# The last output store of a GELU MLP kernel, issued by two engines in two halves of its rows

## The chip, the core and the metric

The kernel runs on one core of a Trainium2 chip. The metric is the device time of one execution in microseconds (us); where several runs are given, their median counts. A core has engines that run side by side and synchronise by semaphores: TensorE (PE, matrix multiplies), VectorE (DVE), ScalarE (ACT), GpSimd (POOL) and SyncE (SP). SP, ScalarE and GpSimd can issue DMAs. An issue occupies the issuing engine's queue for a moment, and the data then moves on DMA engines, 16 for this core, which in this kernel raise a semaphore by 16 for each finished transfer.

## What is computed

The reference is a two-layer perceptron on 2048 tokens with 448 features and 1792 hidden units, in bfloat16:

```python
B, S, D, F = 1, 2048, 448, 1792
h = jnp.einsum("bsd,df->bsf", x, w1) + b1
h = _gelu(h)                       # tanh approximation
return jnp.einsum("bsf,fd->bsd", h, w2) + b2
```

## The kernel before

**Tiles and stages.** Tokens are cut into 4 chunks of 512 and the hidden units into 14 tiles of 128. The first layer (`l1`, matmuls at L260) computes for each pair of chunk and hidden tile a PSUM bank of 128 x 512 sums. ScalarE applies bias and GELU to each of the 56 banks (L360) and writes `g_sb`. The second layer (`l2`, matmuls at L334) takes 16 token tiles of 128 rows in order; for each it adds up 14 matmuls into one PSUM bank of 128 x 448. VectorE adds the bias `b2` to each finished bank (L382) and writes `out_sb`, raising the semaphore `sem_osb` by one.

**The list of outputs.** `outs` holds one entry for each token tile, except that the last tile is cut in two by columns: 0 to 320 and 320 to 448. There are therefore 17 entries. Each is one group of 14 matmuls, one VectorE add and one store. The last entry has 128 columns of 128 rows, in bfloat16 32 KB.

**Loads.** SP issues most of the loads at the start (L204, L205, L178, L183 to L187, L197, L191, L213); ScalarE issues `b1` (L349) and one piece of `w1` (L178), and GpSimd a small filler (L227). All of them are issued before the second layer begins.

**The order of the stores.** The helper `store` (L164 to L167) issues the DMA of one entry from `out_sb` to the output and has it raise `sem_od` by 16. `sync_work` (L203 to L217) has SP wait for each add in turn and issue the first 16 stores:

```python
for n in range(len(outs) - 1):
    sp.wait_ge(sem_osb, n + 1)
    store(sp, n)
sp.wait_ge(sem_od, 16 * len(outs))
```

The last line (L217) is the kernel's final wait: SP waits until all 17 stores have landed, 17 times 16 = 272. The seventeenth store is at the end of `scalar_work`, behind ScalarE's last activation (L364, L365):

```python
act.wait_ge(sem_osb, len(outs))
store(act, len(outs) - 1)
```

So every engine's order is fixed by its program text, and across engines only the semaphores order the work.

Of the kernel before, what the change touches and what calls it, by code (L numbers as in the profile page):

```python
# [11 lines left out]
def bass_standalone__dense_activation_gelu__prompt_kernel(  # L12
# [10 lines left out]
    P = 128  # L23
    HALF = P // 2
# [89 lines left out]
    outs = [(j, 0, D) for j in range(NST - 1)] + [(NST - 1, 0, OCUT), (NST - 1, OCUT, D)]  # L114
# [6 lines left out]
    with ExitStack() as es:  # L121
# [12 lines left out]
        out_sb = sb("out_sb", [P, NST, D], BF16)  # L134
# [22 lines left out]
        sem_osb = S_("sem_osb")  # L157
        sem_od = S_("sem_od")
# [2 lines left out]
        x0_view = x2[0:SC, :].rearrange("(p t) d -> p t d", t=STC)  # L161
        out0_view = out2[0:SC, :].rearrange("(p t) d -> p t d", t=STC)

        def store(eng, n):  # L164
            j, c0, c1 = outs[n]
            to = out0_view[:, j, c0:c1] if j < STC else out2[j * P:(j + 1) * P, c0:c1]
            eng.dma_start(to, out_sb[:, j, c0:c1]).then_inc(sem_od, 16)  # L167

        def x_part(n, parts):
            h, k = parts[0]  # L170
            to = xT_sb[:, k:k + len(parts), 2 * h * P:2 * (h + 1) * P]
            src = ps[XBANK[n]][:, 0:2 * P * len(parts)]
            return to, src.rearrange("p (k t) -> p k t", k=len(parts))

        def load_w10(eng, i):
            a, b = W0_PIECES[i]
            with nc.allow_non_contiguous_dma(reason="w1 column pieces"):
                eng.dma_start(w1_sb[:, 0, a * P:b * P], w1[0:P, a * P:b * P]).then_inc(sem_w10[i], 16)  # L178

        def load_w1(eng):  # L180
            with nc.allow_non_contiguous_dma(reason="w1 column pieces"):
                for k, r in list(enumerate(KROW))[1:]:
                    eng.dma_start(w1_sb[:, k, 0:WCUT], w1[r:r + P, 0:WCUT]).then_inc(sem_w1[k], 16)  # L183
                eng.dma_start(
                    w1_sb[:, 0:3, WCUT:F], w1[0:3 * P, WCUT:F].rearrange("(k p) f -> p k f", p=P)
                ).then_inc(sem_w1r, 16)
                eng.dma_start(w1_sb[:, 3, WCUT:F], w1[KROW[3]:D, WCUT:F]).then_inc(sem_w1r, 16)  # L187

        def load_w2(eng, i):
            a, b = W2_PIECES[i]  # L190
            eng.dma_start(  # L191
                w2_sb[:, a:b, :], w2[a * P:b * P, :].rearrange("(ft p) d -> p ft d", p=P)
            ).then_inc(sem_w2[i], 16)

        def load_xT(eng, c):
            for k, d0 in enumerate(KROW):
                eng.dma_start(  # L197
                    xT_sb[:, k, c * SC:(c + 1) * SC],
                    x2[c * SC:(c + 1) * SC, d0:d0 + P],
                    transpose=True,  # L200
                ).then_inc(sem_x[c], 16)

        def sync_work(sp):  # L203
            sp.dma_start(xn_sb[:, 0:2, :], x0_view[:, 0:2, :]).then_inc(sem_xn[0], 16)  # L204
            sp.dma_start(xn_sb[:, 2:4, :], x0_view[:, 2:4, :]).then_inc(sem_xn[1], 16)  # L205
            load_w10(sp, 1)
            load_w1(sp)
            load_xT(sp, 1)
            for c in range(2, NSC):
                load_xT(sp, c)  # L210
            for i in range(len(W2_PIECES)):
                load_w2(sp, i)
            sp.dma_start(b2_bc[:, :], b2.partition_broadcast(P)).then_inc(sem_b2, 16)  # L213
            for n in range(len(outs) - 1):
                sp.wait_ge(sem_osb, n + 1)
                store(sp, n)
            sp.wait_ge(sem_od, 16 * len(outs))  # L217

        def gpsimd_work(pool):
            pool.memset(ident[:, :], 0.0).then_inc(sem_id, 1)  # L220
# [127 lines left out]
        def scalar_work(act):  # L348
            act.dma_start(b1n_sb[0:NFT, :], b1.rearrange("(c p) -> c p", p=P)).then_inc(sem_b1n, 16)  # L349
            load_w10(act, 0)  # L350
            zero = nc.const_aps.tensor(0.0, [P, 8], FP32)
            act.activation(act_junk[:, :], zero, ACT.Gelu_apprx_tanh)  # L352
            for n, (e, parts) in enumerate(XPARTS):
                if e == "a":
                    act.wait_ge(sem_xtp, n + 1)
                    act.copy(*x_part(n, parts)).then_inc(sem_xTa, 1)  # L356
            act.wait_ge(sem_b1, 1)
            for i, (c, ft) in enumerate(order):
                act.wait_ge(sem_l1, i + 1)
                act.activation(  # L360
                    g_sb[:, ft, c * SC:(c + 1) * SC], bank("g", i)[:, :], ACT.Gelu_apprx_tanh,
                    bias=b1_f[:, ft:ft + 1], scale=1.0,
                ).then_inc(sem_g, 1)
            act.wait_ge(sem_osb, len(outs))  # L364
            store(act, len(outs) - 1)  # L365

        def vector_work(dve):
            for n, (e, parts) in enumerate(XPARTS):
# [17 lines left out]


        sync_work(nc.sync)
        gpsimd_work(nc.gpsimd)
        tensor_work(nc.tensor)  # L390
        scalar_work(nc.scalar)
        vector_work(nc.vector)

# [27 lines left out]
```

## Time and profile before

| what | value |
|---|---|
| median of 3 runs | 94.05 us |
| the runs | 93.27, 94.05, 94.05 us |
| the profiled execution, its own time | 94.23 us |
| its span, first to last instruction | 92.9 us |
| granted TensorE clock | 1.000 |
| second layer's matmuls, L334 | 238, 42.6 us busy, mean 341 ns |
| VectorE's adds, L382 | 17, 10.2 us busy, mean 597 ns |
| store issues on SP, L167 | 16, from 52.0 to 90.8 us, median 332 ns |
| store issue on ScalarE, L167 | 1, at 91.4 us, 358 ns |
| SP's final wait for the landings, L217 | 1.7 us |

How to read it: the span is a part of the execution's own time; 94.23 - 92.9 = 1.33 us lie around it. A row of the timeline begins with the start in us from the span's start and the length in us, then the engine (SPq and ACTq are the DMA issues of SP and ScalarE), the line of the kernel, the operation, and output <- input. A row of the DMA issues ends with how many there were, the KB of each, and the median us from the start of the issue to the landing. In the windows a row begins with the stretch and its length; then come the busy times of PE, PE's weight loads, DVE, ACT and POOL, the granted clock, the busy share of the 16 DMA engines, and the GB/s that they moved. A DMA queue's row has its packets, MB and share of the 16 engines' time: q1 is the queue of SP's DMAs, q10 that of ScalarE's.

### The profile page before, as it was taken

The page shows a single profiled execution, that of the slowest core. Times are in us where ns is not written, and L with a number is a line of the kernel's source. Part 1 is how long each engine was busy: PE and PEld are TensorE (multiplying, and loading weights), DVE is VectorE, ACT ScalarE, POOL GpSimd, SP SyncE. Part 2 cuts the span into 40 slices and gives each one's busy share as a digit, 9 for nine tenths or more (in the row PEclk, how much of TensorE's full clock was granted, in tenths as well). Part 3 has the DMA queues.
Part 4 walks back from the last instruction along what each step waited for, and adds up shares of the span by engine and source line. Part 5 has one row for each costly group of instructions (what it writes and reads, how often), then busy time and mean ns, then how long its engine had stood idle before and what let it go on. Part 6 is the DMA issues. An engine that isn't in the chain of part 4 may idle for free.

```text
span 92.9 us, 1487 instructions
## 1 busy us (share of the span) xinstructions
PE 89.3 (96%) x650; PEld 47.5 (51%) x650; DVE 12.2 (13%) x25; ACT 36.7 (40%) x61; POOL 1.4 (1%) x7
## 2 busy tenths in 40 slices
PE   6968999999999999999999999999999999999991
PEld 4743445555555555555545555555555555555571
DVE  0260000000000000000000222222122222221132
ACT  2640599879777887779776000000000000000000
POOL 5000000000000000000000000000000000000000
DMA  1989965655991000000000110111111101111111
GB/s 34 326 296 347 188 132 96 75 108 91 308 375 46 0 0 4 7 0 0 0 0 0 49 46 10 49 49 49 49 49 49 42 9 55 49 49 49 49 49 49
DMA packets 12562, 7.52 MB, mean 81 GB/s; under 512 B 7171, under 2 KB 12172, under 8 KB 12556
## 3 DMA queue, kind: packets, MB, share of 16 engines
q1 hardware_dynamic: 12208, 7.26, 29.6%
q10 hardware_dynamic: 316, 0.17, 0.6%
q8 instruction: 5, 0.08, 0.3%
q0 software_dynamic: 32, 0.00, 0.0%
q14 instruction: 1, 0.01, 0.0%
HBM read 4.02 MB, written 1.84 MB: 63 GB/s over the span
## 4 chain that ended last, share of the span: by engine, by line
PE 90%; DMA 5%; SPq 1%; DVE 0%; issue 0%
PE ps L334 46%; PE ps L260 44%; DMA wi_sb<-in_w_dram 5%; SPq L178 0%; SPq L205 0%; SPq L204 0%; DVE out_sb L382 0%
## 5 line engine op out<-in xcount | busy, mean ns | idle before, releaser
L260 PE MATMUL ps<-xT_sb,wi_sb 64*128 64x512 bf16 (+2 forms) x384 | 43.0, 374 | 1.0 <-DMA wi_sb<-in_w_dram 1.0
L334 PE MATMUL ps<-wo_sb,g_sb 128*128 128x448 bf16 (+2 forms) x238 | 42.6, 341 | 0.0
L360 ACT ACTIVATE g_sb<-ps,bi_f 128x512 bf16<-128x512 f32 x56 | 33.7, 695 | 10.7 <-PE ps L260 10.7
L334 PEld LDWEIGHTS ps<-wo_sb,g_sb 128*128 128x128 bf16 x238 | 22.7, 98 | 20.1 <-issue 0.4
L260 PEld LDWEIGHTS ps<-xT_sb,wi_sb 64*128 64x128 bf16 (+1 forms) x384 | 21.8, 94 | 21.5 <-DMA wi_sb<-in_w_dram 1.5
L382 DVE TENSOR_TENSOR out_sb<-ps,bo_bc 128x448 bf16<-128x448 f32 (+2 forms) x17 | 10.2, 597 | 74.9 <-PE ps L334 74.9
L233 PE MATMUL ps<-const-bfloat16-1.0 128*128 128x256 bf16 x12 | 2.7, 417 | 0.8 <-PEq L406 0.8
L233 PEld LDWEIGHTS ps<-const-bfloat16-1.0 128*128 128x128 bf16 x12 | 1.7, 144 | 1.4 <-issue 0.8
L352 ACT ACT_TABLE_LOAD x1 | 1.3, 1283 | 1.8 <-issue 1.8
L356 ACT CAST xT_sb<-ps 128x512 bf16<-128x512 f32 (+1 forms) x3 | 1.5, 515 | 1.1 <-PE ps L243 1.1
L371 DVE CAST xT_sb<-ps 128x256 bf16<-128x256 f32 x3 | 1.2, 420 | 4.1 <-PE ps L243 4.1
L243 PE MATMUL ps<-ident,xn_sb 128*128 128x128 bf16 x16 | 1.6, 257 | 0.0
L243 PEld LDWEIGHTS ps<-ident,xn_sb 128*128 128x128 bf16 x16 | 1.3, 117 | 0.4 <-issue 0.4
L376 DVE STREAM_TRANSPOSE bit_sb<-bin_sb 32x32 bf16<-32x32 bf16 x4 | 0.8, 200 | 0.1
L227 POOL DMA_DIRECT2D bin_sb<-in_w_dram x1 | 0.7, 657 | 0.2 <-issue 0.2
L222 POOL TENSOR_SCALAR_AFFINE_SELECT ident<-ident 128x128 bf16<-128x128 bf16 x1 | 0.3, 288 | 0.2 <-POOL ident L220 0.2
L352 ACT ACTIVATE act_junk<-const-float32-0.0 128x8 bf16<-128x8 f32 x1 | 0.2, 209 | 0.0
L220 POOL MEMSET ident<- 128x128 bf16 x1 | 0.2, 204 | 0.3 <-POOLq L406 0.3
L378 DVE CAST bi_f<-bit_sb 128x14 f32<-128x14 bf16 x1 | 0.2, 175 | 0.0
L406 POOL MEMSET const-bfloat16-1.0<- 128x1 bf16 x1 | 0.1, 102 | 0.0
L406 POOL MEMSET const-uint8-127<- 128x1 uint8 x1 | 0.1, 102 | 0.0
L406 POOL MEMSET const-float32-0.0<- 128x1 f32 x1 | 0.1, 98 | 0.2 <-issue 0.2
(1 smaller groups left out, 0.1 us busy)
## 6 DMA issues: line engine op xcount, KB each, us to landing
out_dram<-out_sb SPq DMA_DIRECT2D x15, 112.0 KB, 1.7
wo_sb<-in_w_dram SPq DMA_DIRECT2D x2, 784.0 KB, 5.8
wi_sb<-in_w_dram SPq DMA_DIRECT2D x3, 256.0 KB, 5.2
wi_sb<-in_w_dram SPq DMA_DIRECT2D x1, 576.0 KB, 6.4
xn_sb<-in_x_dram SPq DMA_DIRECT2D x2, 224.0 KB, 2.7
wi_sb<-in_w_dram SPq DMA_DIRECT2D x1, 192.0 KB, 6.5
xT_sb<-in_x_dram SPq DMA_TRANSPOSE x12, 4.2
wi_sb<-in_w_dram ACTq DMA_DIRECT2D x1, 128.0 KB, 3.0
```

Source lines behind the costliest of these rows:

```text
L227: pool.dma_start(b1n_sb[NFT:SQ, :], w1[0:SQ - NFT, 0:P]).then_inc(sem_b1x, 16)
L233: pe.matmul(ps[0][:, 0:WN], lhsT=ones_w, rhs=ones_x, start=True, stop=True)
L243: mm = pe.matmul(ps[XBANK[n]][:, col:col + P], lhsT=xn_sb[:, 2 * h + t, KROW[k]:KROW[k] + P], rhs=ident[:, :], start=True, stop=True,)
L260: return pe.matmul(bank("g", i)[:, t0:t1], lhsT=w1_sb[lo:hi, k, ft * P:(ft + 1) * P], rhs=xT_sb[lo:hi, k, c * SC + t0:c * SC + t1], start= ...
L334: mm = pe.matmul(bank("o", n)[:, 0:c1 - c0], lhsT=g_sb[:, ft, j * P:(j + 1) * P], rhs=w2_sb[:, ft, c0:c1], start=(ft == 0), stop=(ft == NF ...
L352: act.activation(act_junk[:, :], zero, ACT.Gelu_apprx_tanh)
L356: act.copy(*x_part(n, parts)).then_inc(sem_xTa, 1)
L360: act.activation(g_sb[:, ft, c * SC:(c + 1) * SC], bank("g", i)[:, :], ACT.Gelu_apprx_tanh, bias=b1_f[:, ft:ft + 1], scale=1.0,).then_inc( ...
L371: dve.tensor_copy(*x_part(n, parts)).then_inc(sem_xTd, 1)
L376: dve.transpose(b1t_sb[to, :], b1n_sb[:, to]).then_inc(sem_b1T, 1)
L382: dve.tensor_tensor(out=out_sb[:, j, c0:c1], in0=bank("o", n)[:, 0:c1 - c0], in1=b2_bc[:, c0:c1], op=ALU.add,).then_inc(sem_osb, 1)
L406: nc = _bacc.Bacc("TRN2", target_bir_lowering=False, num_devices=1)
```

## The change

The helper `store` takes a range of rows, with all 128 as the default. The first 16 stores are issued as before. Of the seventeenth, SP issues rows 0 to 63 and ScalarE rows 64 to 127; both wait for the same add, the seventeenth rise of `sem_osb`. There are now 18 stores in all, and SP's final wait counts to 18 times 16 = 288.

```diff
-        def store(eng, n):
+        def store(eng, n, p0=0, p1=P):
             j, c0, c1 = outs[n]
             to = out0_view[:, j, c0:c1] if j < STC else out2[j * P:(j + 1) * P, c0:c1]
-            eng.dma_start(to, out_sb[:, j, c0:c1]).then_inc(sem_od, 16)
+            eng.dma_start(to[p0:p1], out_sb[p0:p1, j, c0:c1]).then_inc(sem_od, 16)
...
                 sp.wait_ge(sem_osb, n + 1)
                 store(sp, n)
-            sp.wait_ge(sem_od, 16 * len(outs))
+
+            sp.wait_ge(sem_osb, len(outs))
+            store(sp, len(outs) - 1, 0, HALF)
+            sp.wait_ge(sem_od, 16 * (len(outs) + 1))
...
             act.wait_ge(sem_osb, len(outs))
-            store(act, len(outs) - 1)
+            store(act, len(outs) - 1, HALF, P)
```

## The prediction, made before the changed kernel was run

> **What bounds the kernel now.** I read four views in this order: the page's head and chain of waits, the timeline of the last three microseconds, the windows over the stores' packets, and the timeline of the first two microseconds, where SP and ScalarE already issue DMAs side by side.
>
> The page's head and the chain come first, because they say what a microsecond in any place is worth.
>
> ```profile
> span 92.9 us, 1487 instructions
> PE 89.3 (96%) x650; PEld 47.5 (51%) x650; DVE 12.2 (13%) x25; ACT 36.7 (40%) x61; POOL 1.4 (1%) x7
> ```
>
> ```profile
> 7.20 41.33 PE ps L260 x374
> 48.53 42.53 PE ps L334 x238
> 91.06 0.02 issue
> 91.08 0.29 DVE out_sb L382
> ```
>
> TensorE is the chain from 7.20 to 91.06 us without a break. After it stand one VectorE add of 0.29 us and then the flight of the last store, which the chain does not print but the span contains: the add ends at 91.08 + 0.29 = 91.37 and the span at 92.9. The edit touches nothing before 91.37 us. So the whole stake is the last 1.53 us, 1.6% of 94.05.
>
> The timeline of the tail, and the rows of the DMA issues (KB each, us to landing), show who issues what there.
>
> ```profile
> 90.30 0.49 DVE L382 TENSOR_TENSOR out_sb<-ps,bo_bc 128x320 bf16<-128x320 f32 x1 [1.28 <-PE ps L334]
> 90.82 0.33 SPq L167 DMA_DIRECT2D out_dram<-out_sb  x1
> 91.08 0.29 DVE L382 TENSOR_TENSOR out_sb<-ps,bo_bc 128x128 bf16<-128x128 f32 x1 [0.29 <-PE ps L334]
> 91.40 0.36 ACTq L167 DMA_DIRECT2D out_dram<-out_sb  x1
> ```
>
> ```profile
> out_dram<-out_sb SPq DMA_DIRECT2D x15, 112.0 KB, 1.7
> out_dram<-out_sb SPq DMA_DIRECT2D x1, 80.0 KB, 1.6
> out_dram<-out_sb ACTq DMA_DIRECT2D x1, 32.0 KB, 1.5
> ```
>
> Both stores are issued 0.03 us after their add (90.79 to 90.82 on SP, 91.37 to 91.40 on ScalarE), so neither queue has a backlog. SP's issue ends at 90.82 + 0.33 = 91.15, and from there SP does nothing but wait for the landings; its waits give 1.7 us for that (91.15 to about 92.9). ScalarE's store lands 1.5 us after its issue begins: 91.40 + 1.5 = 92.9, the end of the span.
>
> The windows of 0.1 us split that 1.5 us (last columns: clock, DMA share, GB/s).
>
> ```profile
> 92.00:92.10 0.10, 0.00 (x0) 0.00 (x0) 0.00 (x0) 0.00 (x0) 0.00 (x0) 1.00 0.03 6
> 92.10:92.20 0.10, 0.00 (x0) 0.00 (x0) 0.00 (x0) 0.00 (x0) 0.00 (x0) 1.00 0.00 0
> 92.20:92.30 0.10, 0.00 (x0) 0.00 (x0) 0.00 (x0) 0.00 (x0) 0.00 (x0) 1.00 0.14 36
> 92.30:92.40 0.10, 0.00 (x0) 0.00 (x0) 0.00 (x0) 0.00 (x0) 0.00 (x0) 1.00 0.87 192
> 92.40:92.50 0.10, 0.00 (x0) 0.00 (x0) 0.00 (x0) 0.00 (x0) 0.00 (x0) 1.00 0.47 98
> ```
>
> The last store's packets move from about 92.2 to 92.5. Before them lie 0.8 us from the start of the issue to the first packet, and behind them 0.4 us until the landing is seen. Only about 0.3 of the 1.5 us is data; 1.2 us is a fixed part that any store pays. The 80 KB store's packets are over by 92.1, so SP's queue is empty before the last rows move.
>
> **The change part by part.**
>
> *Removed:* rows 0 to 63 (16 KB) from ScalarE's store. The fixed 1.2 us stays on both halves, since each is a store of its own. What fewer bytes save I take from the three sizes: (1.7 - 1.5) us over (112 - 32) KB is 0.0025 us a KB, so 16 KB less is worth -0.04 us. The best end: if the time of the packets went with the rows of each queue alone, half of 0.3 us would go, -0.15 us; and if the issue of 0.36 us also went with the rows, another -0.18. The rows speak against the second: an issue of 448 columns and one of 320 both take 0.33 us, and ScalarE's 1 KB-wide load took 0.365 against 0.358 for its store. No row here has 64 partitions, so the end of the range stays at -0.33 us. I take -0.04, because the same 32 KB cross the same engines, which are 87% busy at their peak.
>
> On this point the Trainium skill, page "DMA: Bandwidth & Descriptors", section "Rules for kernel authors", advises against two transfers of disjoint partition halves, since both are spread over the same 16 DMA engines and so serialize. The trace's 87% share in the peak window fits it; by the rule the -0.04 us would be nothing, and the sum would be 0.04 us higher.
>
> *Added on SP, wait and issue:* SP gets a wait for the seventeenth add and one DMA issue. SP is free from 91.15, the add is ready at 91.37, so the new wait replaces 0.25 us of the wait for landings. The issue of 0.33 us (the row of the 80 KB store) then stands at 91.40 to 91.73 beside ScalarE's at 91.40 to 91.76 and is not added to it: SP's cover is its final wait until 92.9, behind which nothing is queued. Were that cover gone, SP's own issue would be 0.33 us on the path. SP's half by itself would land at 91.40 + 1.5 - 0.04 = 92.86, with ScalarE's.
>
> *Added, two issues at the same instant:* both engines are released by the same add, which before happened at no store. The nearest rows are at the start.
>
> ```profile
> 0.75 0.66 ACTq L349 DMA_DIRECT2D bin_sb<-in_b_dram  x1
> 1.44 0.36 ACTq L178 DMA_DIRECT2D wi_sb<-in_w_dram  x1
> ...
> 0.75 0.39 SPq L204 DMA_DIRECT2D xn_sb<-in_x_dram  x1
> 1.20 0.41 SPq L205 DMA_DIRECT2D xn_sb<-in_x_dram  x1
> 1.66 0.42 SPq L178 DMA_DIRECT2D wi_sb<-in_w_dram  x1
> ```
>
> They disagree. ScalarE's issue at 1.44 overlaps two of SP's (1.20 to 1.61, 1.66 to 2.08) and took 0.365 us, 0.007 more than the lone one at the end: about +0.01 us. The issues at 0.75 start together, and ScalarE's took 0.66 us, 0.30 more. But that one is also the first DMA of its queue and has 14 rows, so its length has three possible causes; the row at 1.44 has the tile shape of 128 rows and a warm queue. I take +0.01 and keep +0.30 as the upper end; full exclusion would be +0.36, ScalarE's whole issue.
>
> *Added, one more completion:* a store of 128 rows left 144 packets, the 16 above its rows being, I read, what raises the semaphore by 16. So the tail has 16 packets more, one on each of 16 engines. In the window from 90.5 to 93.5 us this queue's row is
>
> ```profile
> q10 hardware_dynamic: 144, 0.03, 5.0%
> ```
>
> and 5.0% of 16 engines' 3.0 us, over 144 packets, is 0.017 us each: +0.02 us. The lower end is nothing.
>
> *Moved:* the final wait counts to 288 and not 272, in the same place; it frees no buffer. No instruction of PE, VectorE or the activations is added or moved, and no load is.
>
> *Sum:* -0.04 + 0.01 + 0.02 = -0.01 us. The profiled execution took 94.23 us, of which 92.9 is the span and 1.33 lies around it; its sum is 94.22. It stands 0.18 us above the median of the runs shown, 94.05, so on that median the sum is 94.04, which I give as 94.0.
>
> **The rivals.**
>
> *The issues exclude each other.* Place: 91.40 us, where one add releases two issues. Price: +0.30 us (0.66 - 0.36) instead of +0.01, so 94.04 + 0.29 = 94.33, say 94.3; it decides if the second issue is held until the first is nearly through. For it speaks the pair at 0.75; against it the overlap at 1.44 at no cost. It would be slower, but by 0.3%.
>
> The Trainium skill, page "Perfetto Trace Analysis", section "DMA Instruction — HWDGE (DVE, Sync)", says that a DMA issue locks a shared descriptor generator for exclusive use. By that rule this rival holds for some part of the issue, which the page gives no time for; the row at 1.44 shows that it is not all of it.
>
> *The rings get in each other's way* (the case that ends slower than 1%). Place: the 16 DMA engines after 92.2, with packets of both queues on each. A ScalarE load of 128 KB amid SP's loads landed only after 3.0 us, 1.5 more than the store at the end. At that price the time is 94.04 + 1.5 = 95.5; it decides from 0.95 us of stretch. Against it: that load shared the engines with hundreds of KB, here both halves together are 32 KB, and the last two stores of before, 0.58 us apart and in flight together, landed in 1.6 and 1.5 us. The 16 KB of the other half at the slope above are 0.04 us.
>
> *The halves land sooner.* Price -0.15 us for packets, up to -0.33 with shorter issues: 93.9 to 93.7. For it: only the 0.3 us of data shrinks with the work, and no row of 64 partitions excludes it. Against: the 0.8 us before and the 0.4 us behind the packets are fixed. Over 1% faster would need 0.94 of 1.5 us, more than everything that could shrink.
>
> **How the numbers follow.** Forecast, nothing to speak of (94.0): 0.56. Exclusion at issue (94.3): 0.30. Sooner (93.7 to 93.9): 0.09. Rings in the way (95.5): 0.05. The three runs of before lie between 93.27 and 94.05, 0.8% apart, wider than any case but the last; a measurement of this kernel can hardly tell less than 1% from no change. The range therefore goes from 93.3, where the lowest run lies, to 94.6, which is the exclusion's full +0.36 (94.4) with 0.2 of that scatter. It holds all but the last case and about a tenth from scatter.
>
> Beyond 1%, that is below 93.11 or above 94.99: faster 0.04, from scatter alone, added to a small gain; slower 0.09, of which 0.05 is the rings' case and 0.04 scatter on the exclusion; within 1%: 0.87.
>
> **What would show it right or wrong.** In the timeline of the changed kernel two store issues should stand at about 91.4 us, on SP and ScalarE, of 0.33 and 0.36 us; one of 0.5 us or more, or one that starts late, is exclusion. The DMA rows should show 16.0 KB twice, landing in 1.45 to 1.5 us; 1.3 us or less is the sooner case, 2 us or more the rings' case. Packets from both queues should lie between 92.2 and 92.5, SP's queue having 80 more of them and ScalarE's 80 in place of 144. The PE rows and the start of the last add must be as before. The prediction is wrong if the span differs by more than 0.4 us with PE's rows unchanged, or if something ahead of 91.37 us moves, which nothing in the edit gives a reason for.

## The result and the profile after

Over 22 runs of each kernel the median is 94.22 us after (93.60 to 95.36) against 93.92 us before (93.27 to 94.45). The ratio is 1.0046, 95% interval [1.0024, 1.0068], with one disturbed run of the changed kernel left out of it. The change costs 0.43 us (0.0046 times 93.92), with an interval from 0.23 to 0.64. That is within 1%, but it is clear of zero, and it is a loss. The medians themselves lie 0.30 us apart, inside this interval. The prediction had said 94.0 and no difference to speak of.

The profiled execution of the changed kernel took 94.74 us, of which the span is 93.4 and 1.34 us lie around it. First its chain, to see whether anything ahead of the last store moved:

```profile
span 93.4 us, 1488 instructions
PE 90.2 (97%) x650; PEld 48.1 (51%) x650; DVE 12.2 (13%) x25; ACT 36.7 (39%) x61; POOL 1.4 (1%) x7
```

```profile
48.51 42.53 PE ps L337 x238
91.03 0.02 issue
91.06 0.29 DVE out_sb L385
```

The second layer again takes 42.53 us and the last add begins at 91.06 instead of 91.08 us (the lines are numbered 3 higher). PE's busy total is 0.9 us higher than before, but the second layer starts no later, at 48.51 against 48.53 us. Up to the end of this add, 91.35 us, nothing is slower. The tail behind it has grown from 92.9 - 91.37 = 1.53 us to 93.4 - 91.35 = 2.05 us: +0.52 us, within the measured interval. All of the loss lies here, so this is the place to read line by line. The timeline of the changed kernel from 91.2 us on:

```profile
91.06 0.29 DVE L385 TENSOR_TENSOR out_sb<-ps,bo_bc 128x128 bf16<-128x128 f32 x1 [0.29 <-PE ps L337]
91.38 0.55 SPq L167 DMA_DIRECT2D out_dram<-out_sb  x1
91.38 0.55 ACTq L167 DMA_DIRECT2D out_dram<-out_sb  x1
```

and the rows of its last DMA issues (number, KB, us from issue to landing):

```profile
out_dram<-out_sb SPq DMA_DIRECT2D x1, 80.0 KB, 1.6
...
out_dram<-out_sb SPq DMA_DIRECT2D x1, 16.0 KB, 1.8
out_dram<-out_sb ACTq DMA_DIRECT2D x1, 16.0 KB, 2.0
```

The two issues begin together at 91.38 us, as foreseen. But both take 0.55 us, where issues of twice the rows took 0.33 on SP and 0.36 on ScalarE, and the halves land after 1.8 us (SP's) and 2.0 us (ScalarE's), where the whole store landed after 1.5. The new last landing is 91.38 + 2.0 = 93.4 us, the end of the span. Where the packets lie is shown by the DMA view in two windows, first from 92.1 to 92.82 us, then from 92.82 to 93.4:

```profile
DMA packets 80, 0.02 MB, mean 23 GB/s; under 512 B 80, under 2 KB 80, under 8 KB 80
...
q1 hardware_dynamic: 80, 0.02, 12.0%
```

```profile
DMA packets 80, 0.02 MB, mean 28 GB/s; under 512 B 80, under 2 KB 80, under 8 KB 80
...
q10 hardware_dynamic: 80, 0.02, 14.5%
```

All 80 packets of SP's queue come before 92.82 us and all 80 of ScalarE's behind it. The two halves do not run side by side: they run one after the other, and the first already starts late. In the kernel before, packets began 0.8 us behind the issue; here the first ones begin in the slice from 92.5 us, 1.1 to 1.2 us behind it:

```profile
92.40:92.50 0.10, 0.00 (x0) 0.00 (x0) 0.00 (x0) 0.00 (x0) 0.00 (x0) 1.00 0.00 0
92.50:92.60 0.10, 0.00 (x0) 0.00 (x0) 0.00 (x0) 0.00 (x0) 0.00 (x0) 1.00 0.12 26
```

Two theories stood at this point. **A:** two engines that issue at the same instant get in each other's way (the prediction's rival of exclusion, and what its own list of signs would have called this). **B:** the halves are slow because of what they are, two stores of 64 rows, whoever issues them and when.

### The profile page after: what moved, and what is told of

Same layout as the page of the kernel before. It is cut to its first block, busy times and chain, and to the rows that moved or that the text cites. A ratio compares the mean times of both kernels' runs of the same rounds, so it can differ in the third digit from the quotient of the medians.

```text
span 93.4 us, 1488 instructions
## 1 busy us (share of the span) xinstructions
PE 90.2 (97%) x650; PEld 48.1 (51%) x650; DVE 12.2 (13%) x25; ACT 36.7 (39%) x61; POOL 1.4 (1%) x7
## 4 chain that ended last, share of the span: by engine, by line
PE 97%; DVE 0%; issue 0%
PE ps L263 46%; PE ps L337 46%; PE ps L236 3%; PE ps L246 2%; DVE out_sb L385 0%
## 5 line engine op out<-in xcount | busy, mean ns | idle before, releaser
L236 PE MATMUL ps<-const-bfloat16-1.0 128*128 128x256 bf16 x12 | 2.7, 417 | 0.8 <-PEq L409 0.8
L236 PEld LDWEIGHTS ps<-const-bfloat16-1.0 128*128 128x128 bf16 x12 | 1.7, 144 | 1.4 <-issue 0.8
L246 PE MATMUL ps<-ident,xn_sb 128*128 128x128 bf16 x16 | 2.1, 309 | 0.0
L230 POOL DMA_DIRECT2D bin_sb<-in_w_dram x1 | 0.7, 655 | 0.2 <-issue 0.2
```

The costliest lines, as they stand in the source:

```text
L230: pool.dma_start(b1n_sb[NFT:SQ, :], w1[0:SQ - NFT, 0:P]).then_inc(sem_b1x, 16)
L236: pe.matmul(ps[0][:, 0:WN], lhsT=ones_w, rhs=ones_x, start=True, stop=True)
L246: mm = pe.matmul(ps[XBANK[n]][:, col:col + P], lhsT=xn_sb[:, 2 * h + t, KROW[k]:KROW[k] + P], rhs=ident[:, :], start=True, stop=True,)
```

## Experiments

**One engine issues both halves.** SP's new wait and store go away; ScalarE issues both:

```diff
-            sp.wait_ge(sem_osb, len(outs))
-            store(sp, len(outs) - 1, 0, HALF)
             sp.wait_ge(sem_od, 16 * (len(outs) + 1))
...
             act.wait_ge(sem_osb, len(outs))
+            store(act, len(outs) - 1, 0, HALF)
             store(act, len(outs) - 1, HALF, P)
```

Expected: 

> Both halves of the last store are issued by ScalarE, one after the other; SP issues neither. If the cost comes from two engines issuing at the same instant, each issue takes 0.36 us as in the kernel before, the second begins 0.36 us after the first, and the second lands about 1.85 us after the first issue began (0.36 + 1.5): 0.36 us later than before, and 0.15 to 0.2 sooner than the 2.02 us of the change. If the cost comes from two small stores being in flight on the same DMA engines, the second half's own landing is longer than 1.6 us here too.

Measured: the ratio to before is 1.0090 [1.0057, 1.0122]. No other engine issues anything here, and still the timeline shows, in two windows at the two starts,

```profile
90.87 0.53 ACTq L167 DMA_DIRECT2D out_dram<-out_sb  x1
```

```profile
91.44 0.60 ACTq L167 DMA_DIRECT2D out_dram<-out_sb  x1
```

The issues are as long as in the change and longer, and they land after 1.8 us. Theory A had said 0.36. The total is later than in the change, since the second issue waits for the first.

**One half alone.** SP's half is left out altogether; ScalarE stores rows 64 to 127.

```diff
-            sp.wait_ge(sem_osb, len(outs))
-            store(sp, len(outs) - 1, 0, HALF)
-            sp.wait_ge(sem_od, 16 * (len(outs) + 1))
+            sp.wait_ge(sem_od, 16 * len(outs))
```

Expected: 

> ScalarE stores rows 64 to 127 of the last tile as in the change, and rows 0 to 63 of its last 128 columns are not stored at all. If the cost comes from issuing at the same instant, the issue is back at 0.36 us and the landing at 1.45 to 1.5 us. If a store of 64 rows is slow by itself, the issue stays near 0.55 us and the landing near 2.0 us.

Measured, from one execution (timeline, then the row of the DMA issues):

```profile
90.53 0.53 ACTq L167 DMA_DIRECT2D out_dram<-out_sb  x1
```

```profile
out_dram<-out_sb ACTq DMA_DIRECT2D x1, 16.0 KB, 1.8
```

This is the run that decides against A as the main cause. With nothing beside it, the store of half the rows still takes an issue of 0.53 us and lands after 1.8 us: 0.3 us later than the store of all the rows. Of these 0.3 us the issue itself explains only 0.17 (0.53 against 0.36); the rest lies behind the issue.

**The whole store on SP.** ScalarE's store goes away, SP stores all 128 rows.

```diff
-            store(sp, len(outs) - 1, 0, HALF)
-            sp.wait_ge(sem_od, 16 * (len(outs) + 1))
+            store(sp, len(outs) - 1)
+            sp.wait_ge(sem_od, 16 * len(outs))
...
-            act.wait_ge(sem_osb, len(outs))
-            store(act, len(outs) - 1, HALF, P)
```

Expected: 

> The whole last store of 128 rows on SP, nothing on ScalarE. Every theory expects an issue of 0.33 us and a landing of 1.5 us, so the time of the kernel before within 0.05 us. Should SP be a slow place for a store right behind its 80 KB store, the landing would be 1.8 us as for SP's half in the change.

Measured: ratio 0.9996 [0.9965, 1.0026], an issue of 0.33 us and a landing after 1.5 us. SP is not a slow place for a store right behind its 80 KB store, so SP's 1.8 us in the change is not that either.

**Two issues at one instant, without the split.** The kernel before, with a load of 64 rows issued by SP beside ScalarE's whole store:

```diff
+            sp.wait_ge(sem_osb, len(outs))
+            sp.dma_start(junk[0:HALF, :], w2[0:HALF, 0:P]).then_inc(sem_junk, 16)
             sp.wait_ge(sem_od, 16 * len(outs))
+            sp.wait_ge(sem_junk, 16)
```

Expected: 

> ScalarE issues the whole last store as in the kernel before; SP, released by the same add, issues a load of 64 rows of 128 elements into an unused tile, and waits for it at the end. The store itself is not split. If two issues at one instant slow each other, ScalarE's issue is near 0.55 us, its store lands after 1.7 to 2.1 us, and the time is 0.2 to 0.6 us above before. If splitting the store is what costs, the issue is 0.36 us, the landing 1.5 us, and the time is that of before.

Measured:

```profile
90.83 0.55 SPq L220 DMA_DIRECT2D junk<-in_w_dram  x1
90.84 0.35 ACTq L169 DMA_DIRECT2D out_dram<-out_sb  x1
```

```profile
out_dram<-out_sb ACTq DMA_DIRECT2D x1, 32.0 KB, 1.5
junk<-in_w_dram SPq DMA_DIRECT2D x1, 16.0 KB, 2.2
```

The total, 1.0090 [1.0059, 1.0122], is 0.84 us above before (0.0090 times 93.74), with an interval from 0.55 to 1.14. That is more than the 0.2 to 0.6 us that A had given, but far from no change, and read alone it would have spoken for A. The lines say otherwise. ScalarE's store of 128 rows is untouched by its neighbour, 0.35 us and 1.5 us; the time is lost by the load, which ends the kernel because it is waited for. The load is the DMA with 64 rows. It is also a load, so a slow issue of 64 rows is not seen with stores alone. How long a load of other rows takes at this place was not tried; SP's loads of 128 rows at the start of the kernel before took 0.39 to 0.49 us.

**The same two engines, the same instant, cut by columns.** Each stores all 128 rows, 64 columns of them.

```diff
-            store(sp, len(outs) - 1, 0, HALF)
+            store(sp, len(outs) - 1, 0, OCUT + (D - OCUT) // 2)
...
-            store(act, len(outs) - 1, HALF, P)
+            store(act, len(outs) - 1, OCUT + (D - OCUT) // 2, D)
```

(the two last arguments are columns here).

Expected: 

> The last store is split between SP and ScalarE as in the change, at the same instant, but by columns: each stores all 128 rows, 64 columns of them. If 64 rows in a DMA are what is slow, the issues are 0.33 and 0.36 us, both land after 1.5 to 1.6 us and the time is that of before within 0.1 us. If two issues at one instant are what costs, the issues are near 0.55 us, the landings 1.8 to 2.0 us and the time is 0.3 to 0.5 us above before, as in the change.

Measured: ratio 1.0020 [0.9985, 1.0055], and

```profile
90.78 0.33 SPq L168 DMA_DIRECT2D out_dram<-out_sb  x1
90.79 0.37 ACTq L168 DMA_DIRECT2D out_dram<-out_sb  x1
```

with landings after 1.4 and 1.6 us. Two stores of 16 KB, issued by two engines at one instant, cost about what one of 32 KB does: from the end of the last add to the end of the span it is 1.65 us (92.4 - 90.75), where it was 1.53 before and 2.05 in the change. What is left of B is the number of rows.

**Cut at other rows.** The change with SP taking rows 0 to 15, and with SP taking rows 0 to 31:

```diff
-            store(sp, len(outs) - 1, 0, HALF)
+            store(sp, len(outs) - 1, 0, 16)
...
-            store(act, len(outs) - 1, HALF, P)
+            store(act, len(outs) - 1, 16, P)
```

(and 32 in place of 16).

Expected, cut at 16: 

> The change with another cut: SP stores rows 0 to 15 of the last 128 columns, ScalarE rows 16 to 127, at the same instant. If the cost belongs to DMAs of 64 rows in particular, both issues take 0.31 to 0.36 us, both land after 1.4 to 1.55 us and the time is that of before within 0.1 us. If it belongs to any cut by rows issued at one instant, issues near 0.55 us, a landing of 1.8 to 2.0 us and 0.3 to 0.5 us more than before.

Expected, cut at 32: 

> The change cut at row 32: SP rows 0 to 31, ScalarE rows 32 to 127 (96 rows). If 64 rows are the only slow number, issues of 0.32 and 0.36 us, landings up to 1.55 us and the time of before within 0.1 us. In the run of shapes an issue of 96 rows took 0.43 us, but it came 0.66 us behind one of 64; if 96 rows are slow by themselves, ScalarE's issue is 0.43 us or more here and the landing 1.6 us or more.

Measured: ratios 1.0008 [0.9975, 1.0041] and 0.9989 [0.9954, 1.0024]. Cut at 32, the timeline, the landings, and the queues between 92.3 and 92.7 us are

```profile
91.53 0.35 SPq L167 DMA_DIRECT2D out_dram<-out_sb  x1
91.53 0.38 ACTq L167 DMA_DIRECT2D out_dram<-out_sb  x1
```

```profile
out_dram<-out_sb ACTq DMA_DIRECT2D x1, 24.0 KB, 1.5
out_dram<-out_sb SPq DMA_DIRECT2D x1, 8.0 KB, 1.4
```

```profile
q10 hardware_dynamic: 112, 0.02, 29.4%
q1 hardware_dynamic: 48, 0.01, 11.3%
```

This is the change itself with one number altered, and the loss is gone. All 160 packets of both queues lie in one stretch of 0.4 us; of those in its middle, from 92.42 to 92.54 us, 72 are ScalarE's and 30 SP's, so the queues overlap. Cut at 16 the issues are 0.35 and 0.38 us too, with landings after 1.3 and 1.5 us. The intervals of the totals are wide: the one of the cut by columns reaches up to 1.0055 and the one of the cut at 16 up to 1.0041, so by the total alone only the cut at 32 speaks clearly against a loss of 0.0046. The lines decide: the stretch behind the last add is 1.6 us in both cuts by rows (92.1 - 90.51 and 93.1 - 91.50).

**The shapes by themselves.** The last store is as before; in the middle of the second layer, where SP has time, it stores some token tiles in parts of many shapes. A sample of the edit:

```diff
+                if n == 4:
+                    sp.dma_start(o3[0:64, 4, :], out_sb[0:64, 4, :]).then_inc(sem_od, 16)
+                    sp.wait_ge(sem_l2, n + 2)
+                    sp.dma_start(o3[64:128, 4, :], out_sb[64:128, 4, :]).then_inc(sem_od, 16)
```

Expected: 

> The last store is as in the kernel before. In the middle of the second layer, off the path that sets the end, SP stores token tiles 4 to 12 in parts of other shapes, each issued apart from the others: 64+64, 96+32 and 112+16 rows of 448 columns, 128 rows in 320+128 columns, 64+64 rows over two tiles at once (128 runs of 448 columns in each), 64+64 rows of 128 columns, 128 rows of 128 and 192 columns, and two whole tiles. If the number of rows decides, every part with fewer than 128 rows takes an issue of 0.5 us or more and every one with 128 takes 0.33. If the number of contiguous runs decides, the parts with 64 rows over two tiles take 0.33 us as well. If bytes decide, the parts with 128 and 192 columns are slow.

Expected, a second run with parts 2.65 us apart: 

> The last store is as in the kernel before. In the middle of the second layer SP stores token tiles 4 to 8 in parts, one part behind each add, so 2.65 us apart: rows 0-63, 64-127, 0-47, 48-127, 0-71, 72-127, 32-95, 0-31, 96-127, 0-119, 120-127. If 64 rows in particular are slow, the three parts of 64 rows take 0.47 to 0.55 us, wherever they begin, and all others 0.31 to 0.36. If instead a first DMA of a new shape is slow, the second and third part of 64 rows are quicker than the first and the parts of 48, 80, 72 and 56 rows are slow too.

Measured in the first of the two; the lines are, in order, 64 and 64 rows (L218, L220), 96 and 32 (L222, L224), 112 and 16 (L226, L228), 128 rows of 128 columns (L232), 64 rows over two tiles (L234, L236), 64 rows and then 128 rows of 128 columns (L240, L242):

```profile
61.53 0.55 SPq L218 DMA_DIRECT2D out_dram<-out_sb  x1
63.52 0.47 SPq L220 DMA_DIRECT2D out_dram<-out_sb  x1
64.18 0.43 SPq L222 DMA_DIRECT2D out_dram<-out_sb  x1
66.17 0.33 SPq L224 DMA_DIRECT2D out_dram<-out_sb  x1
66.83 0.32 SPq L226 DMA_DIRECT2D out_dram<-out_sb  x1
68.82 0.31 SPq L228 DMA_DIRECT2D out_dram<-out_sb  x1
...
71.47 0.35 SPq L232 DMA_DIRECT2D out_dram<-out_sb  x1
74.84 0.65 SPq L234 DMA_DIRECT2D out_dram<-out_sb  x1
76.77 0.61 SPq L236 DMA_DIRECT2D out_dram<-out_sb  x1
...
79.41 0.49 SPq L240 DMA_DIRECT2D out_dram<-out_sb  x1
80.07 0.46 SPq L242 DMA_DIRECT2D out_dram<-out_sb  x1
```

and in the second, 64 and 64 rows (L220, L222), 48 and 80 (L224, L226), 72 and 56 (L228, L230), rows 32 to 95 (L232), 120 and 8 rows (L238, L240):

```profile
61.71 0.56 SPq L220 DMA_DIRECT2D out_dram<-out_sb  x1
64.36 0.47 SPq L222 DMA_DIRECT2D out_dram<-out_sb  x1
67.00 0.35 SPq L224 DMA_DIRECT2D out_dram<-out_sb  x1
69.65 0.32 SPq L226 DMA_DIRECT2D out_dram<-out_sb  x1
72.30 0.35 SPq L228 DMA_DIRECT2D out_dram<-out_sb  x1
74.95 0.32 SPq L230 DMA_DIRECT2D out_dram<-out_sb  x1
...
77.60 1.43 SPq L232 DMA_DIRECT2D out_dram<-out_sb  x1
...
85.54 0.35 SPq L238 DMA_DIRECT2D out_dram<-out_sb  x1
...
88.19 0.30 SPq L240 DMA_DIRECT2D out_dram<-out_sb  x1
```

Issues of 8, 16, 32, 48, 56, 72, 80, 112, 120 and 128 rows take 0.30 to 0.36 us, apart from one of 128 explained below; those of 64 rows take 0.47 or more, wherever they begin, and rows 32 to 95 took 1.43. My expectation for the first of the two runs was wrong in part: not every part under 128 rows is slow. Neither contiguous runs (two tiles of 64 rows have 128 of them and took 0.61 and 0.65) nor bytes decide. The first DMA with 64 rows of each run is 0.08 to 0.09 us longer than the second, but the second is still slow, so it is not a matter of a first use. (The first was rows 0 to 63 and the second rows 64 to 127 in both runs, so the 0.08 us may belong to the place of the rows.) The 96 rows at 0.43 us come 0.66 us behind a DMA of 64; a part of 128 rows and 128 columns that came 0.66 us behind another one took 0.46 us (L242), though the same shape by itself took 0.35 (L232). So in both cases what was issued shortly behind a DMA of 64 rows paid 0.05 to 0.11 us as well, and with the 0.38 us in the cut at row 32, 96 rows are not slow by themselves.

**Who pays for the second half?** A half alone landed after 1.8 us, but ScalarE's in the change after 2.0. To see which of the two is late, SP was given fulfilled waits ahead of its store:

```diff
             sp.wait_ge(sem_osb, len(outs))
+            for _ in range(8):
+                sp.wait_ge(sem_osb, len(outs) - 1)
             store(sp, len(outs) - 1, 0, HALF)
```

Expected: 

> The change, but SP passes eight more waits that are already fulfilled before it issues its half, so that it comes some 0.3 to 0.5 us after ScalarE's. ScalarE's half should now land after 1.8 us, as when it was alone, and not 2.0. If the two halves are handled one after the other, SP's, coming second, lands after 1.8 us or more from its own issue. If 64 rows had nothing to do with it and only the common instant did, both issues would be 0.36 us.

Expected, with three waits: 

> As the run with eight waits, with three, so that SP's issue comes some 0.1 to 0.2 us after ScalarE's and still overlaps it. ScalarE's half should land after about 1.8 us and SP's after 1.9 to 2.1: whichever is first is served as if alone, and the other pays the 0.2 us more.

Measured: the waits are far cheaper than I had thought. Three moved nothing: SP still issues first (90.75 against 90.76 us), its half lands after 1.8 us and ScalarE's after 2.0, the change once more. Eight moved SP by 0.07 us, enough to reverse the order:

```profile
91.16 0.55 ACTq L167 DMA_DIRECT2D out_dram<-out_sb  x1
91.23 0.55 SPq L167 DMA_DIRECT2D out_dram<-out_sb  x1
```

```profile
out_dram<-out_sb ACTq DMA_DIRECT2D x1, 16.0 KB, 1.8
out_dram<-out_sb SPq DMA_DIRECT2D x1, 16.0 KB, 2.0
```

Now ScalarE's half lands after 1.8 us and SP's after 2.0. So the 0.2 us belong to whichever of two 64-row stores comes second, not to an engine or a queue. A stagger wide enough to keep the halves apart was not reached.

## Why the prediction was wrong

**The step that failed** is the one headed *Removed*. It carried the fixed part of the whole store, 1.2 of 1.5 us, over to the halves unchanged, and on the shape it said "No row here has 64 partitions, so the end of the range stays at -0.33 us. I take -0.04", that is, it bounded a shape that the trace did not show on the side of a gain only, and let fewer rows cost less or the same. A half alone costs 0.3 us more than the whole (1.8 against 1.5 us), and the part that was taken as fixed is what grew: in the change the first packet comes 1.1 to 1.2 us behind the issue, where it came after 0.8. The same omission sits in the step on SP's issue, which took "0.33 us (the row of the 80 KB store)", a row of 128 partitions; it was 0.55.

**Two issues at the same instant.** The step took +0.01 us and kept +0.30 as its end. For issues of other shapes the small value was right: in the cuts at 16 and 32 rows they took 0.35 and 0.38 us, 0.02 over 0.33 and 0.36, by columns 0.33 and 0.37, and ScalarE's whole store beside the load 0.35, no longer than alone. What the Trainium skill, page "Perfetto Trace Analysis", section "DMA Instruction — HWDGE (DVE, Sync)", says of a generator that is locked for exclusive use fits these runs with a price of at most about 0.02 us; no run shows the lock itself. The 0.2 us by which the second 64-row store lands later do not stand in its issue, which took 0.55 us like the first one's; they lie behind it. Taken together, these terms of the sum are -0.04 + 0.01 in the prediction, and +0.3 for a half by itself with +0.2 for standing second in the runs: 0.5 us, where the measurement shows 0.43 [0.23, 0.64].

**The rival of exclusion** was priced at 94.3 us, close to the measured 94.22, but its mechanism is refuted: a half without any neighbour had an issue of 0.53 us, and a 128-row store with a neighbour one of 0.35. Its price came from the first issue of ScalarE, 0.66 us, whose cause is still open. The prediction's own sign for it, "one of 0.5 us or more", could not tell the rival from a slow shape. A sign that is seen in both engines at once should have been doubted: of two that exclude each other, one goes first and takes its usual time.

**The other rivals.** The prediction's sign for the rings' case, a landing after 2 us or more, was just met by ScalarE's half, but two queues with packets in flight together are not the cause: in the cut at row 32 both queues' packets lie in the same 0.4 us and land after 1.4 and 1.5 us. Landing sooner is true of one part alone (4 KB after 1.3 us, 8 KB and SP's 16 KB of the cut by columns after 1.4), which helps nothing while the other part lands after 1.5 or 1.6. The advice of the Trainium skill, page "DMA: Bandwidth & Descriptors", section "Rules for kernel authors", against two transfers of disjoint partition halves is borne out as far as there is no gain in any of the cuts; that the halves come strictly one after the other is seen only where they have 64 rows.

**What held.** The stake is the tail alone; the chain up to the last add did not move. Both engines issue at the same instant, 0.03 us behind the add. SP's issue is covered by its final wait. The packets are 80 and 80, though they come from 92.5 us on and not between 92.2 and 92.5. The extra completions, put at up to 0.02 us, are too small to be told apart in the cuts, which all have them. The time lies within the range and within 1%, but as far as the mechanism goes that is luck: the upper end of the range came from the rival of exclusion, whose mechanism is refuted. No loss was forecast, and there is one. By one of the prediction's own signs, too, it was wrong: the span differs by 0.5 us (93.4 - 92.9) with the second layer's 42.53 us unchanged, more than the 0.4 that it allowed.

**What stays open.** Why 64 rows are slow, in the issue and behind it, and why rows 32 to 95 took 1.43 us (one issue, not repeated), no view of the trace shows. All the numbers of rows tried in stores are multiples of 8, and all but 64 behave alike; others were not tried.

No version beat the kernel before: the whole store on SP, the cut by columns and the cuts at 16 and 32 rows are all the same as before within their intervals.

## What to carry to other kernels

Splitting a transfer into two that start together took nothing off the fixed part, here 1.2 of 1.5 us, in any of the cuts, so there was little to win at the end of this kernel. A DMA of a shape that the trace does not show can be slower than one of twice its size: bound an unseen shape on both sides, and measure one issue of it off the critical path, as the runs of shapes do, before it is put on the path. When a total agrees with a theory, read the lines as well: the run with the extra load had a total that spoke for theory A and the lines of theory B.

## What the runs showed of the hardware

- A DMA issue with 64 rows took 0.47 to 0.65 us on SP and 0.53 to 0.60 on ScalarE, against 0.30 to 0.38 for stores of eleven other numbers of rows from 8 to 128 that did not follow shortly behind one of 64. At the end of the kernel, with 128 columns, a store of 64 rows landed after 1.8 us against 1.5 for 128 rows. The one load of 64 rows took 0.55 us to issue.
- One issue of rows 32 to 95 took 1.43 us.
- Two issues 0.66 us behind one of 64 rows were 0.05 and 0.11 us longer than issues of these rows elsewhere (0.43 us for 96 rows, 0.38 on ScalarE in the cut at 32; 0.46 for 128 rows, 0.35 by itself).
- Two 64-row stores issued together: the first landed after 1.8 us, the second after 2.0, whichever engine was first, with no overlap of their packets.
- Two issues of other shapes at the same instant on SP and ScalarE lengthened each other by at most about 0.02 us.
- Eight fulfilled semaphore waits on SP delayed its next issue by no more than about 0.07 us.
